# A linear-attention kernel with a two-layer block: transposes of q and k moved from TensorE to crossbar DMA, a scheduler that models the DMA queue, and one token chunk loaded between the halves of a weight

## The chip, the cores and the metric

One core of one Trainium2 chip. The metric is the device time of one execution in microseconds (us); a profiled execution also gives a span, from its first to its last instruction, some 2 to 5 us shorter than the times of the unprofiled runs. Ratios compare kernels that ran in turn on the same chip.

The core's engines are TensorE (PE in the profile; PEld is its weight load), VectorE (DVE), ScalarE (ACT), GpSimd (POOL) and SyncE (SP), which here only issues transfers. "SPq" is SyncE's in-order queue of transfers. The core has two on-chip memories: here TensorE's results land in PSUM and are copied from there to SBUF, where the other operands lie. "The mask" below is VectorE's multiplication of the scores by the causal mask.

## The reference

Batch 4, 8 heads, 768 positions, head size 64. Decaying linear attention by blocks, then two dense layers with a smooth rectifier between them:

```python
for b in range(nb):                       # blocks of 64 positions
    intra = einsum('bhic,bhjc->bhij', qb, kb) * Dmask
    intra = einsum('bhij,bhjd->bhid', intra, vb)
    inter = einsum('bhid,bhde->bhie', qb * lam_pow, kv_state)
    out[:, :, sl] = intra + inter
    kv_state = lam_block * kv_state + einsum('bhsd,bhse->bhde', kb * rev_pow, vb)
x = out.transpose(0, 2, 1, 3).reshape(3072, 512)
h = x @ w_in                              # 512 x 2048
g = where(h >= 1, h, where(h <= -1, 0, (h + 1)**2 / 4))
y = g @ w_out                             # 2048 x 512
```

## The kernel before

The 3072 tokens are 24 chunks of 128 (six per batch element), and four chunks make a stripe of 512. Each chunk is loaded as three transfers of 256 KB (k, q, v), cast to bf16 with the decay factor multiplied in, transposed, and taken through scores (`s`), mask (`m`), output (`o`) and state update (`u`). Each stripe then goes through layer one (`l1`), the rectifier (`r` on ScalarE, `g` on VectorE) and layer two (`l2`).

Casts, transposes and the copies out of PSUM that follow them:

```python
def cast(c, x, eng):                      # eng: GpSimd, except four casts of the first chunks
    tab, d, nm = ((tab_q, qs, "qs"), (tab_k, ks, "ks"))[x]
    t = qkp.tile([128, H, D], BF16, name=nm, tag=nm)
    eng.tensor_tensor(t, qkv_ld[c, x], _bc(tab[:, c % NCB, :], 2, D), op=AX.mult)

def f_t(c):                               # 8 transposes on TensorE
    ptt[c] = pp_t.tile([128, 2, HP, 128], BF16, name="pt", tag="pt")
    for i, x in ((1, ks), (0, qs)):
        for hp in range(HP):
            nc.tensor.transpose(out=ptt[c][:, i, hp, :], in_=pair(x[c], hp), identity=ident)

def f_kb(c, hi):
    nc.vector.tensor_copy(kbd[c % NKB][HD[hi], :, hi, :], ptt[c][HD[hi], 1])

def f_qT(c, e):
    qT[c] = qtp.tile([128, HP, 128], BF16, name="qT", tag="qT")
    (nc.scalar.copy if e == "ACT" else nc.vector.tensor_copy)(qT[c], ptt[c][:, 0])
```

The program is not written in its final order. Each step is an operation with an engine, an assumed duration, needs and a due time; a list scheduler (`run_plan`), run when the kernel is built, puts them in order. Before, a transfer is an operation of a made-up engine "DMA" that does one at a time:

```python
add(("ld", i, x), "DMA", 1190, ..., [("cast", i - LD, x), ...], extra=1400, due=pos_)
...                                       # loads: chunks 0-3, w_in (4 quarters), chunk 4, w_out (4), the rest
t, e = min((max(free[e], min(r for r, _ in lst)), e) for e, lst in ready.items() if lst)
free[e] = t + x.ns
x.t, x.end = t, t + x.ns + x.extra
```

## Time and profile before

| | before |
|---|---|
| median of 4 runs | 239.69 us (238.71 to 240.53) |
| span of the profiled execution | 234.8 us |
| TensorE, VectorE, GpSimd busy | 213.8, 160.3, 59.4 us |
| TensorE waits after 50 us that the profile names | 1.5 us |
| DMA engines full until | about 123 us |

The lines behind this are in the prediction below. How to read such a page: busy time is the union of an engine's instructions and says only how full it is. Whether time there is worth anything is decided by the windows (is the engine full in that stage?) and by the waits (what ended its idle time?). Matmul records can be missing (before: 1876 recorded, 1904 weight loads), so a small hole in TensorE is a wait only if the list of waits names it.

### The profile page before, as it was taken

The page shows a single profiled execution, that of the slowest core. Times are in us where ns is not written, and L with a number is a line of the kernel's source. Part 1 is how long each engine was busy: PE and PEld are TensorE (multiplying, and loading weights), DVE is VectorE, ACT ScalarE, POOL GpSimd, SP SyncE. Part 2 cuts the span into 40 slices and gives each one's busy share as a digit, 9 for nine tenths or more (in the row PEclk, how much of TensorE's full clock was granted, in tenths as well). Part 3 has the DMA queues.
Part 4 walks back from the last instruction along what each step waited for, and adds up shares of the span by engine and source line. Part 5 has one row for each costly group of instructions (what it writes and reads, how often), then busy time and mean ns, then how long its engine had stood idle before and what let it go on. Part 6 is the DMA issues. An engine that isn't in the chain of part 4 may idle for free.

```text
span 234.8 us, 4665 instructions
## 1 busy us (share of the span) xinstructions
PE 213.8 (91%) x1876; PEld 137.1 (58%) x1904; DVE 160.3 (68%) x274; ACT 123.4 (53%) x216; POOL 59.4 (25%) x64
## 2 busy tenths in 40 slices
PE   0487997999997999999999999999999999999993
PEld 0476633575896997777765455555555454444441
DVE  7587399957499999885776876876766835545300
ACT  3456566243577766666566366566455354544110
POOL 6562071061366548303303403302000000000000
PEclk9999999999999999999999999999999999999999
DMA  6999969986999999899993011011011011110212
GB/s 139 220 212 200 192 112 185 196 162 186 247 201 218 227 221 206 191 243 228 230 255 81 19 45 37 12 45 47 0 45 47 0 45 47 45 43 2 92 51 83
DMA packets 82725, 29.67 MB, mean 126 GB/s; under 512 B 75536, under 2 KB 79632, under 8 KB 82704
## 3 DMA queue, kind: packets, MB, share of 16 engines
q1 hardware_dynamic: 78336, 25.17, 48.2%
q0 software_dynamic: 4224, 4.19, 11.1%
q8 instruction: 15, 0.25, 0.4%
q14 instruction: 6, 0.05, 0.1%
q10 hardware_dynamic: 144, 0.00, 0.0%
HBM read 27.27 MB, written 6.29 MB: 143 GB/s over the span
## 4 chain that ended last, share of the span: by engine, by line
PE 75%; DVE 16%; ACT 3%; DMA 2%; issue 2%; SPq 0%; ACTq 0%
PE py L323 33%; PE ph L295 26%; PE ps L252 5%; DVE gT L315 4%; PE pt L229 4%; PE po L268 4%; DMA x2f<-in_v_dram 2%; DVE sc L258 2%; PE pu L242 2%; PE po L265 2%; ACT r L303 1%; DVE kbd_121 L232 1%; PE ph L288 1%; DVE kbd_120 L232 1%; DVE qT L236 1%
## 5 line engine op out<-in xcount | busy, mean ns | idle before, releaser
L303 ACT ACTIVATE r<-ph,one 128x512 bf16<-128x512 f32 x94 | 64.1, 687 | 57.6 <-PE ph L295 40.9
L295 PE MATMUL ph<-xT,w_in_sb 128*128 128x128 bf16 (+1 forms) x744 | 93.1, 269 | 1.0 <-ACT r L303 0.4
L323 PE MATMUL py<-w_out_sb,gT 128*128 128x512 bf16 x364 | 91.5, 379 | 0.9
L295 PEld LDWEIGHTS <-w_in_sb 128*128 128x128 bf16 x752 | 53.0, 98 | 28.0 <-issue 1.4
L323 PEld LDWEIGHTS <-gT 128*128 128x128 bf16 x384 | 35.4, 98 | 33.3 <-DVE gT L315 0.2
L219 POOL TENSOR_TENSOR ks<-x1f,tab_k 128x512 bf16<-128x512 f32 x21 | 24.0, 1141 | 93.0 <-DMA x1f<-in_k_dram 38.9
L258 DVE TENSOR_TENSOR sc<-ps,causal 128x512 bf16<-128x512 f32 x48 | 33.0, 687 | 19.0 <-PE ps L252 18.8
L219 POOL TENSOR_TENSOR qs<-x0f,tab_q 128x512 bf16<-128x512 f32 x23 | 25.8, 1123 | 7.0 <-DMA x0f<-in_q_dram 6.9
L328 ACT COPY osb<-py 128x512 f32<-128x512 f32 x24 | 14.1, 586 | 20.6 <-PE py L323 20.0
L275 ACT CAST xT<-po 128x512 bf16<-128x512 f32 x24 | 14.0, 585 | 11.9 <-PE po L268 11.8
L242 PEld LDWEIGHTS <-ks 128*128 128x128 bf16 x80 | 6.2, 105 | 9.7 <-DVE ks L219 7.1
L229 PE MATMUL pt<-ident,ks 128*128 128x128 bf16 x96 | 10.1, 232 | 0.1
L229 PE MATMUL pt<-ident,qs 128*128 128x128 bf16 x96 | 10.0, 231 | 0.0
L229 PEld LDWEIGHTS <-ks 128*128 128x128 bf16 x96 | 7.7, 106 | 3.3 <-issue 0.3
L252 PE MATMUL ps<-qT,kbd_121 128*128 128x128 bf16 x64 | 6.8, 229 | 3.0 <-DVE qT L236 1.7
L242 PE MATMUL pu<-vi_126,ks 128*128 128x128 bf16 x24 | 2.5, 232 | 7.7 <-ACT vi_126 L223 7.7
L236 DVE COPY qT<-pt 128x512 bf16<-128x512 bf16 x20 | 8.5, 425 | 0.3
L252 PEld LDWEIGHTS <-kbd_121 128*128 128x128 bf16 x64 | 4.9, 102 | 5.8 <-DVE kbd_121 L232 2.6
L252 PE MATMUL ps<-qT,kbd_120 128*128 128x128 bf16 x64 | 6.8, 229 | 1.4 <-ACT qT L236 1.1
L232 DVE COPY kbd_120<-pt 64x512 bf16<-64x512 bf16 x16 | 6.7, 418 | 1.7 <-PE pt L229 0.9
L252 PE MATMUL ps<-qT,kbd_122 128*128 128x128 bf16 x64 | 6.5, 225 | 1.3 <-DVE qT L236 0.8
L252 PEld LDWEIGHTS <-kbd_120 128*128 128x128 bf16 x64 | 4.8, 102 | 3.8 <-DVE kbd_120 L232 1.8
(207 smaller groups left out, 246.4 us busy)
## 6 DMA issues: line engine op xcount, KB each, us to landing
x1f<-in_k_dram SPq DMA_DIRECT2D x24, 256.0 KB, 4.6
x0f<-in_q_dram SPq DMA_DIRECT2D x24, 256.0 KB, 4.8
x2f<-in_v_dram SPq DMA_DIRECT2D x24, 256.0 KB, 4.7
out_dram<-osb SPq DMA_DIRECT2D x24, 256.0 KB, 2.0
w_in_sb<-in_moe_w_in_dram POOLq DMA_DIRECT2D x4, 512.0 KB, 8.3
w_out_sb<-in_moe_w_out_dram POOLq DMA_DIRECT2D x4, 512.0 KB, 8.3
lam_b<-in_lam_dram ACTq DMA_DIRECT2D x1, 4.0 KB, 3.3
```

The costliest lines, as they stand in the source:

```text
L219: eng.tensor_tensor(t, qkv_ld[c, x], _bc(tab[:, c % NCB, :], 2, D), op=AX.mult)
L229: nc.tensor.transpose(out=ptt[c][:, i, hp, :], in_=pair(x[c], hp), identity=ident)
L232: nc.vector.tensor_copy(kbd[c % NKB][HD[hi], :, hi, :], ptt[c][HD[hi], 1])
L236: (nc.scalar.copy if e == "ACT" else nc.vector.tensor_copy)(qT[c], ptt[c][:, 0])
L242: nc.tensor.matmul(pu[0][:, hp, :], lhsT=pair(ks[c], hp), rhs=v_pair(vi[c % NV], hp), start=(c % NCB == 0 and hp == 0), stop=True, skip_gr ...
L252: nc.tensor.matmul(pst[c, g][:, 2 * j + hi, :], lhsT=kbd[c % NKB][:, 2 * g + j, hi, :], rhs=qT[c][:, 2 * g + j, :], start=True, stop=True)
L258: nc.vector.tensor_tensor(sc_sb[c][:, 4 * g:4 * g + 4, :], pst[c, g], _bc(causal, 1, 4), op=AX.mult)
L275: nc.scalar.copy(out=xT[sx][:, :, off:off + C], in_=pot[c])
L295: nc.tensor.matmul(ph[:, j * m:(j + 1) * m], lhsT=w_in_sb[:, ko, (ni + j) * 128:(ni + j + 1) * 128], rhs=xT[s][:, ko, part * m:(part + 1) ...
L303: nc.scalar.activation(out=r_t[grp][:, i, :], in_=ph_t[s, ni, part], func=AF.Relu, bias=one[:, 0:1])
L323: nc.tensor.matmul(py_t[s, ms], lhsT=gT[s][:, ko, ms * 128:(ms + 1) * 128], rhs=w_out_sb[:, ko, :], start=(ko == 0), stop=(ko == FO - 1))
L328: nc.scalar.copy(out=osb[s, ms], in_=py_t[s, ms])
```

## The change

Five things, meant to take work off TensorE and to let the scheduler judge when a transfer lands:

1. Chunks 6 to 23 (`XT = 6`) are transposed by the DMA crossbar (a transfer that writes its data transposed), two transfers of 128 KB per chunk, issued by SyncE. Their `qT` copy goes; the two half copies of `kbd` read SBUF.
2. The scheduler models the queue: SyncE issues (`SP`, with its own time), at most three transfers of it are unfinished (`RING = 3`), all share one DMA time line.
3. Chunk 4's loads move from behind `w_in` to between its halves, and the second half of `w_in` is issued after the cast of chunk 4's k.
4. TensorE's order in stripe 0 is fixed (`seq0`); one group of scores gets another PSUM bank; three early parts of layer one instead of four.
5. Four instead of three buffers for the cast and the transposed q and k.

```diff
+    XT, NQT, NQK, RING = 6, 4, 4, 3
+    ORDER = [(0, 0), (0, 1), 4, (0, 2), (0, 3), (1, 0), (1, 1), (1, 2), (1, 3)]
...
+            self.extra = dma + 2700 - ns if dma else extra
...
+            t, e = min((max(free[e], min(r for r, _ in lst), xfer[-RING] if e == "SP" else 0), e)
+                       for e, lst in ready.items() if lst)
...
+            if x.dma:
+                dma_free = max(dma_free, t + 1300) + x.dma
+                x.end = dma_free + 1400
+                if e == "SP":
+                    xfer.append(dma_free)
...
     def f_kb(c, hi):
-        nc.vector.tensor_copy(kbd[c % NKB][HD[hi], :, hi, :], ptt[c][HD[hi], 1])
+        nc.vector.tensor_copy(kbd[c % NKB][HD[hi], :, hi, :], ptt[c][HD[hi], 1] if c < XT else kT[c][HD[hi]])
+    def f_kx(c):
+        kT[c] = qtp.tile([128, HP, 128], BF16, name="kT", tag="kT")
+        nc.sync.dma_start_transpose(out=kT[c], in_=ks[c].rearrange("p h d -> p (h d)"))
+    def f_qx(c):
+        qT[c] = qtp.tile([128, HP, 128], BF16, name="qT", tag="qT")
+        nc.sync.dma_start_transpose(out=qT[c], in_=qs[c].rearrange("p h d -> p (h d)"))
...
+            add(("t", c), "SP", 1200, lambda c=c: f_kx(c), [...], due=-2, dma=860)
+            add(("qT", c), "SP", 1200, lambda c=c: f_qx(c), [...], due=-2, dma=860)
...
+    for x, y in zip(seq0, seq0[1:]):
+        OPS[y].keys.append(x)
```

More of the change, by code (lines that the diff above doesn't have):

```diff
@@ L62 @@
     ld = ctx.enter_context(tc.tile_pool(name="ld", bufs=LD))
-    qkp = ctx.enter_context(tc.tile_pool(name="qkp", bufs=3))
-    qtp = ctx.enter_context(tc.tile_pool(name="qtp", bufs=3))
+    qkp = ctx.enter_context(tc.tile_pool(name="qkp", bufs=NQK))
+    qtp = ctx.enter_context(tc.tile_pool(name="qtp", bufs=NQT))
     scp = ctx.enter_context(tc.tile_pool(name="scp", bufs=3))
@@ L155, with __init__, add @@
     class Op:
-        def __init__(self, key, eng, ns, fn, needs, due, extra):
-            self.key, self.eng, self.ns, self.fn, self.keys, self.own, self.extra = key, eng, ns, fn, needs, due, extra
-    def add(key, eng, ns, fn, needs=(), due=None, extra=0):
-        OPS[key] = Op(key, eng, ns, fn, needs, due, extra)
+        def __init__(self, key, eng, ns, fn, needs, due, extra, dma):
+            self.key, self.eng, self.ns, self.fn, self.keys, self.own, self.dma = key, eng, ns, fn, needs, due, dma
+            self.extra = dma + 2700 - ns if dma else extra
+    def add(key, eng, ns, fn, needs=(), due=None, extra=0, dma=0):
+        OPS[key] = Op(key, eng, ns, fn, needs, due, extra, dma)
         ops.append(OPS[key])
@@ L178, in run_plan @@
         for x in reversed(topo):
-            d = [u.due - u.ns - x.extra - LAT for u in users[x.key] if u.eng != "DMA"]
+            d = [u.due - u.ns - x.extra - LAT for u in users[x.key] if not u.dma]
             x.due = min(d + ([x.own] if x.own is not None else []), default=1e9)
-            if x.eng == "DMA" or x.key[0] in ("l1", "l2"):
+            if x.dma or x.key[0] in ("l1", "l2"):
                 x.due = x.own
@@ L187, in run_plan @@
                 ready[x.eng].append((0, x))
-        out_seq = []
+        out_seq, xfer, dma_free = [], [0] * RING, 0
         while len(out_seq) < len(ops):
-            t, e = min((max(free[e], min(r for r, _ in lst)), e) for e, lst in ready.items() if lst)
+            t, e = min((max(free[e], min(r for r, _ in lst), xfer[-RING] if e == "SP" else 0), e)
+                       for e, lst in ready.items() if lst)
             r, x = min(((r, x) for r, x in ready[e] if r <= t), key=lambda p: (p[1].due, p[0]))
@@ L206, in mm @@
         return sum(c / 2.4 + 3 for c in cols)
-    qs, ks, qT, sc_sb, xT, ptt, pst, pot = {}, {}, {}, {}, {}, {}, {}, {}
+    qs, ks, kT, qT, sc_sb, xT, ptt, pst, pot = {}, {}, {}, {}, {}, {}, {}, {}, {}
     pu = [None]
@@ L248, in f_s @@
     def f_s(c, g):
-        pst[c, g] = pp_s.tile([128, 4, 128], F32, name="ps", tag="ps")
+        pl, nm = (pp_h, "ph") if (c, g) == (CPS - 1, 1) else (pp_s, "ps")
+        pst[c, g] = pl.tile([128, 4, 128], F32, name=nm, tag=nm)
         for j in range(2):
@@ L283, in f_l1 @@
             if split == 0:
-                pl, nm = (pp_h, "ph") if ni < 2 else (pp_y, "py")
+                pl, nm = (pp_h, "ph") if ni == 0 else (pp_y, "py")
                 ph_t[s, ni, part] = pl.tile([128, MS], F32, name=nm, tag=nm)
@@ L367, in f_load @@
         qkv_ld[c, x] = t
-    order = [("c", c) for c in range(CPS)] + [("w", 0), ("c", CPS), ("w", 1)] + [("c", c) for c in range(CPS + 1, NCH)]
-    pos_ = 0
-    for kind, i in order:
-        if kind == "w":
-            for j in range(WS):
-                add(("wi", i, j), "POOL", 900, lambda i=i, j=j: (load_w_in, load_w_out)[i](j),
-                    [("cast", CPS - 2 + min(j, 1), 0), ("cast", CPS - 2 + min(j, 1), 1), ("wi", i, j - 1)] if i == 0 else [("cast", CPS, 1), ("cast", CPS, 0) if j else None, ("wi", i, j - 1)],
-                    due=j + 4 * i)
-                add(("w", i, j), "DMA", 3100, lambda: None, [("wi", i, j), ("ld", CPS - 1, 2) if i == 0 else ("ld", CPS, 1)], extra=1500, due=pos_)
-                pos_ += 1
+    order = list(range(CPS)) + ORDER
+    order += [c for c in range(CPS, NCH) if c not in order]
+    w_seen, last_c, pos_ = [], None, 0
+    for it in order:
+        if isinstance(it, tuple):
+            lead = [("cast", CPS - 2, 0), ("cast", CPS - 2, 1)] if not w_seen else [("cast", last_c, 1)]
+            add(("w",) + it, "POOL", 900, lambda it=it: (load_w_in, load_w_out)[it[0]](it[1]),
+                lead + [("w",) + w_seen[-1]] if w_seen else lead, due=pos_ * 1e-3, dma=3100)
+            w_seen.append(it)
+            pos_ += 1
             continue
+        gated = len(w_seen) - 2 if last_c is not None and w_seen and not isinstance(order[order.index(it) - 1], int) else None
         for x in (1, 0, 2):
-            wait = {CPS: WS - 2, CPS + 1: 2 * WS - 2}.get(i) if x == 1 else None
-            add(("ld", i, x), "DMA", 1190, lambda i=i, x=x, wait=wait: f_load(i, x, wait),
-                [("cast", i - LD, x), ("w", int(i > CPS), WS - 2) if i >= CPS else None], extra=1400, due=pos_)
+            add(("ld", it, x), "SP", 590, lambda i=it, x=x, wait=gated if x == 1 else None: f_load(i, x, wait),
+                [("cast", it - LD, x), ("w",) + w_seen[-2] if w_seen else None], due=pos_ * 1e-3, dma=1190)
             pos_ += 1
+        last_c = it
     for c in range(NCH):
@@ L393 @@
                 lambda c=c, x=x, eng=(nc.vector if e == "DVE" else nc.gpsimd): cast(c, x, eng),
-                [("ld", c, x), ("t", c - 3), ("u", c - 3), ("cast", c - 1, x)])
+                [("ld", c, x), ("cast", c - 1, x), ("t", c - NQK), ("u", c - NQK) if x else ("qT", c - NQK)])
         add(("cast", c, 2), "ACT", 640, lambda c=c: cast_v(c),
             [("ld", c, 2), ("o", c - NV), ("u", c - NV), ("cast", c - 1, 2)])
-        add(("t", c), "PE", mm(*[128] * 8), lambda c=c: f_t(c),
-            [("cast", c, 0), ("cast", c, 1), ("kb", c - 1, 0), ("kb", c - 1, 1), ("qT", c - 1)], due=od - 6000, extra=FILL)
+        if c < XT:
+            add(("t", c), "PE", mm(*[128] * 8), lambda c=c: f_t(c),
+                [("cast", c, 0), ("cast", c, 1), ("kb", c - 1, 0), ("kb", c - 1, 1), ("qT", c - 1)], due=od - 6000, extra=FILL)
+            e = "ACT" if c < CPS else "DVE"
+            add(("qT", c), e, 600 if c < CPS else 365, lambda c=c, e=e: f_qT(c, e), [("t", c), ("o", c - NQT), ("qT", c - 1)])
+        else:
+            add(("t", c), "SP", 1200, lambda c=c: f_kx(c), [("cast", c, 1), ("kb", c - NQT, 0), ("kb", c - NQT, 1)], due=-2, dma=860)
+            add(("qT", c), "SP", 1200, lambda c=c: f_qx(c), [("cast", c, 0), ("o", c - NQT)], due=-2, dma=860)
         for hi in range(2):
-            add(("kb", c, hi), "DVE", 365, lambda c=c, hi=hi: f_kb(c, hi), [("t", c), ("s", c - NKB, 1)])
-        e = "ACT" if c < CPS else "DVE"
-        add(("qT", c), e, 600 if c < CPS else 365, lambda c=c, e=e: f_qT(c, e), [("t", c), ("o", c - 3), ("qT", c - 1)])
+            add(("kb", c, hi), "DVE", 365 if c < XT else 285, lambda c=c, hi=hi: f_kb(c, hi), [("t", c), ("s", c - NKB, 1)])
         if cb < NCB - 1:
@@ L409 @@
             add(("s", c, h), "PE", mm(*[128] * 4), lambda c=c, h=h: f_s(c, h),
-                [("kb", c, 0), ("kb", c, 1), ("qT", c), ("m", c, 0) if h else ("m", c - 1, 1)],
+                [("kb", c, 0), ("kb", c, 1), ("qT", c), (("m", c, 0) if c != CPS - 1 else None) if h else ("m", c - 1, 1) if c != CPS else ("m", c - 1, 0)],
                 due=od - 3000 + 1000 * h, extra=FILL)
@@ L421 @@
     l2_order = [x for x in l_seq if x[0] == 2]
-    NA = 4
+    NA = 3
     for i in range(NA):
@@ L433 @@
             lambda a=(s, i, n, p, 1 if n1 < NA else None): f_l1(*a),
-            kx + [("w", 0, (i + n - 1) * WS // FO), ("la", n1) if n1 < NA else ("r", n1 - (4 if n1 < NA + 2 else 2)), ("l1", n1 - 1)], due=l_due[1, s, i, p], extra=FILL)
+            kx + [("w", 0, (i + n - 1) * WS // FO), ("la", n1) if n1 < NA else ("r", 0 if n1 == NA + 1 else n1 - 2) if n1 > NA else ("m", CPS - 1, 1), ("l1", n1 - 1)], due=l_due[1, s, i, p], extra=FILL)
         add(("r", n1), "ACT", 690, lambda a=(s, i, n, p, grp, j): f_r(*a),
@@ L449 @@
             add(("y", y), "ACT", 600, lambda a=(s, ms): f_y(*a), [("l2", n2), ("y", y - 1), ("st", y - 3)])
-            add(("st", y), "DMA", 780, lambda a=(s, ms): f_st(*a), [("y", y), ("st", y - 1)], extra=1400, due=-1)
-    run_plan({"PE": 7000, "ACT": 6500, "DVE": 6000, "POOL": 7000, "DMA": 2000})
+            add(("st", y), "SP", 550, lambda a=(s, ms): f_st(*a), [("y", y), ("st", y - 1)], due=-1, dma=780)
+    seq0 = [("u", 0), ("t", 0), ("s", 0, 0), ("t", 1), ("s", 0, 1), ("u", 1), ("o", 0)]
+    for c in range(1, CPS):
+        seq0 += [("s", c, 0), ("t", c + 1), ("s", c, 1)] + ([("u", c + 1)] if c < CPS - 2 else []) + [("o", c)] if c < CPS - 1 else [
+            ("s", c, 0), ("s", c, 1), ("la", 0), ("la", 1), ("o", c), ("la", 2), ("l1", 0), ("l1", 1), ("l1", 2), ("l1", 3), ("u", c)]
+    for x, y in zip(seq0, seq0[1:]):
+        OPS[y].keys.append(x)
+    run_plan({"PE": 7000, "ACT": 6500, "DVE": 6000, "POOL": 7000, "SP": 800})
 _INS = ['q', 'k', 'v', 'lam', 'moe_w_in', 'moe_w_out']
```

## The prediction

> **What bounds the kernel now.** I read the page's first two parts, then the windows by stage, then the waits of TensorE, and last the timelines of TensorE and of the two queues that issue transfers. The page of the kernel before says this (engines with busy time, share and count; then forty slices of 5.87 us each, in tenths):
>
> ```profile
> span 234.8 us, 4665 instructions
> PE 213.8 (91%) x1876; PEld 137.1 (58%) x1904; DVE 160.3 (68%) x274; ACT 123.4 (53%) x216; POOL 59.4 (25%) x64
> ...
> PE   0487997999997999999999999999999999999993
> ...
> DMA  6999969986999999899993011011011011110212
> GB/s 139 220 212 200 192 112 185 196 162 186 247 201 218 227 221 206 191 243 228 230 255 81 19 45 37 12 45 47 0 45 47 0 45 47 45 43 2 92 51 83
> ```
>
> TensorE is full from about the eighth slice to the end, the DMA engines are full only up to slice 21, some 123 us. So two things are busy together in the first half and only one in the second. Which of them sets the end is seen in the windows (busy time and count for PE, PEld, DVE, ACT, POOL; then clock, DMA share, GB/s):
>
> ```profile
> 0.00:7.67 7.67, 0.00 (x1) 0.10 (x1) 5.29 (x11) 2.48 (x5) 5.67 (x13) 1.00 0.81 159
> 7.67:20.00 12.33, 9.63 (x85) 8.48 (x85) 8.76 (x15) 6.66 (x14) 6.49 (x8) 1.00 1.32 212
> 20.00:30.00 10.00, 8.33 (x80) 5.63 (x81) 4.58 (x9) 5.60 (x11) 0.00 (x0) 1.00 1.12 197
> 30.00:50.00 20.00, 17.93 (x142) 10.43 (x143) 17.33 (x28) 10.13 (x17) 7.66 (x8) 1.00 0.98 174
> 50.00:70.00 20.00, 19.89 (x244) 15.27 (x244) 14.75 (x24) 11.42 (x21) 7.94 (x8) 1.00 0.92 194
> 70.00:80.00 10.00, 8.72 (x139) 7.89 (x138) 9.74 (x18) 7.06 (x14) 5.47 (x5) 1.00 1.00 212
> 80.00:140.00 60.00, 59.06 (x659) 42.95 (x668) 48.82 (x86) 36.46 (x66) 20.04 (x18) 1.00 0.81 177
> 140.00:220.00 80.00, 79.53 (x493) 41.64 (x501) 51.02 (x89) 41.20 (x68) 6.13 (x6) 1.00 0.09 34
> ```
>
> From 50 us on TensorE has hardly a hole. Part of the 1.28 us missing in 70 to 80 is not a wait: groups of w_out matmuls stand there as three records where the program has four. The waits say it better: from 50 to 230 us TensorE waits 1.5 us in all (0.8 for qT, 0.5 and 0.2 for sc, all three made by VectorE). Between 20 and 50 us it waits 3.8 us, of which this is the largest item:
>
> ```profile
> PE ps L252 <- DVE qT L236: 1.7, 1, 1.7
> ```
>
> From 7.67 us (first matmul) to 20 us it is short of work and its 128-column matmuls come 107 ns apart rather than 56. At the end some 4 us go by after the last matmul (last copy, last store). So the kernel is: about 8 us of start, 40 us with holes, 180 us of TensorE without holes, 4 us of tail. The transfers are full but ahead: the last load is issued at 120.8 us, while the last transposes of these data run at 181.9 us.
>
> **What the Trainium skill says.** "TensorE: Matmul & The Clock Gate", § Wait — 56ns, not 53.3ns?, gives N/2.4 GHz + 2.5 ns for warm back-to-back matmuls, 55.6 ns at 128 columns and 215.7 at 512, and 106.7 ns for 128 columns cold. The trace agrees: four 128-column transposes start 0.22 us before what follows, four 512-column matmuls take 0.86 us, and the cold groups before 19 us take 0.43 us for four. "VectorE: DVE Perf Modes", § The three transpose paths, puts a 128x128 bf16 transpose at 390 ns on TensorE against 1309 ns by the DMA crossbar; the trace before has no crossbar transpose, and its TensorE transposes, pipelined, cost a seventh of the 390. "DMA: Bandwidth & Descriptors", § Latency and other measured facts, gives 261 GB/s for DMA transposes with a non-contiguous middle dimension; no run here shows it yet. The VectorE page, § Why PSUM operands drop a tier, says that a PSUM operand keeps a copy out of the mode that uses both SBUF read ports. Here copies out of PSUM take 0.42 us for 512 columns; the SBUF form is not in the trace.
>
> **The change part by part.**
>
> *Transposes off TensorE.* Chunks 6 to 23, 18 of 24, no longer use it for transposing. The rows of the removed work and of the copies after it:
>
> ```profile
> L229 PE MATMUL pt<-ident,ks 128*128 128x128 bf16 x96 | 10.1, 232 | 0.1
> L229 PE MATMUL pt<-ident,qs 128*128 128x128 bf16 x96 | 10.0, 231 | 0.0
> L236 DVE COPY qT<-pt 128x512 bf16<-128x512 bf16 x20 | 8.5, 425 | 0.3
> ```
>
> The 232 ns is the latency of one, and the 20 us busy time counts it overlapped; what TensorE gains is the spacing, 56 ns. Removed are 18 x 8 = 144 transposes, 144 x 0.0558 = **8.0 us**. All of these lie after 50 us in the order of the old program, where TensorE waits for nothing, so they come off the end almost whole. (They are the last 144 of 192, the later six-eighths.)
>
> *VectorE.* 18 copies of qT go (18 x 0.425 = 7.7 us). The 36 half copies of kbd stay, but read SBUF; if they fall from 0.42 to 0.29 us, the number that the new scheduler assumes, that is 36 x 0.13 = 4.7 us. Together 12 of 160 us. VectorE is not the bound, but it is 97% busy from 70 to 80, and the 1.5 us of TensorE waits after 50 us are all on it. I take **0.8 us** from this.
>
> *Transfers added.* 36 transposes of 128 KB each. At the page's 261 GB/s one is 0.5 us; the scheduler in the diff assumes 0.86 us of transfer and 1.2 us on the issuing queue. I estimate 36 x 0.86 = 31 us of DMA and 43 us of queue. Loads now pass at about one per 1.1 to 1.2 us, so a chunk costs 3.6 us of DMA now, and some 5.3 us plus a store (2 us to landing) after. TensorE uses a stripe of four chunks per some 33 us in the second half, 8 us per chunk. So the transfers, spread to some 150 us instead of 123, still run ahead. The narrow place is chunks 8 to 12: the old kernel consumes them between 79 and 98 us, 4.7 us each, faster than 5.3 us; but it casts chunk 8 at 64 us, a lead of 15 us. I charge **1.5 us** for new waits, mostly here.
>
> *Start.* Chunk 4's loads come after the first half of w_in, not the whole. Before, they are issued at 26.5 us, when the third quarter has landed:
>
> ```profile
> 26.50 0.37 SPq L364 DMA_DIRECT2D x1f<-in_k_dram  x1
> 26.91 0.58 SPq L364 DMA_DIRECT2D x0f<-in_q_dram  x1
> 27.54 1.40 SPq L364 DMA_DIRECT2D x2f<-in_v_dram  x1
> 43.87 0.37 SPq L364 DMA_DIRECT2D x1f<-in_k_dram  x1
> ```
>
> Weights land some 3.1 us apart (my estimate from first issue at 14.1 us and third landing at 26.4), so the first quarter is in at about 20.2 us and chunk 4 arrives some 5 us earlier. That can remove the 1.7 us wait at 40 us. The price: quarters three and four of w_in are issued after the cast of chunk 4's k, so I estimate the third at 31 to 32 us; the ninth block of the first layer, which reads it, starts at 31.4 us now. Order on TensorE in stripe 0 hardly changes: score group two of chunk 3 gets another PSUM bank, three early parts instead of four, one state update put back. Of 3.8 us waited in 20 to 50, I take **1.8 us** net.
>
> *Sum:* 240.1 - 8.0 - 0.8 - 1.8 + 1.5 = **231.2 us**, 3.7% less.
>
> **Rivals.** (1) *The queue becomes the wait.* Loads, stores and transposes share one in-order queue; a transpose waiting for a cast holds the loads behind it. For it: even before, the queue stands from 48.3 to 53.2 us on a store with a load behind. Against it: six load buffers and the lead of 15 us. If transposes cost double (2 us each of queue and DMA), a chunk is some 8 us, about what TensorE needs, and chunks 8 to 12 come late by 5 to 8 us: 236 to 239 us. (2) *The late w_in half stalls stripe 0.* That would eat the gain of the start and up to 3 us more: 233 to 235. (3) *Hidden anyway:* if something other than TensorE set the pace after 50 us, removing the transposes would give nothing, some 239; the 1.5 us of waits speak strongly against it. (4) *All works,* with the holes of 20 to 80 us closed too: 228.
>
> **Range and chances.** The arithmetic of the 8.0 us is firm; the terms around it are each 1 to 3 us. The range is 228 to 236.5 us. "Faster by over 2%" begins below 235.3 us, so the new waits may eat up to four of the nine microseconds: chance 0.83. Within 2%: 0.14, mainly rival 1. Slower: 0.03, if transposes take several microseconds each.
>
> **What would show it.** Right: TensorE with 144 fewer matmuls and some 300 fewer instructions with their weight loads, still full from 50 us on; span near 226; DMA full until 145 to 155 us; VectorE near 148 us; half copies of kbd clearly under 0.42 us. Wrong: TensorE waits on kbd or qT of chunks 6 to 12 summing to several us, or slices 9 to 16 of TensorE under 9; a wait on w_in near 31 us; transposes that take over 1.5 us each of queue or of DMA; VectorE copies no shorter.

## More of the kernel before

The rectifier on VectorE has three instructions for each group of 1024 columns, all with operands in SBUF only; the mask reads PSUM:

```python
nc.vector.tensor_scalar(t, r, 0.5, 1.0, op0=AX.mult, op1=AX.min)
nc.vector.tensor_tensor(w, r, t, op=AX.subtract)
nc.vector.tensor_tensor(gT[...], w, t, op=AX.mult)
...
nc.vector.tensor_tensor(sc_sb[c][:, 4*g:4*g+4, :], pst[c, g], _bc(causal, 1, 4), op=AX.mult)   # mask
```

## The result

The changed kernel takes **232.22 us** (median of 4 runs, 231.14 to 233.71) against 239.69; its result is correct. The ratio is 0.9694, 95% interval 0.9625 to 0.9764. A ratio is the mean time of one kernel's runs over that of the other's of the same rounds, so not quite the ratio of the medians. Executions over 1.5% slower than the fastest of the same kernel are left out of the means. Run again on another chip (first experiment below) the ratio was 0.9739 (0.9696 to 0.9782). So the change saves 6 to 7.5 us.

The page of the changed kernel, the lines that answer to those of before:

```profile
span 229.4 us, 4429 instructions
PE 207.1 (90%) x1756; PEld 127.4 (56%) x1756; DVE 159.9 (70%) x256; ACT 123.5 (54%) x216; POOL 63.3 (28%) x64
...
PE   0497969999999998988999998999999999999993
...
DMA  6999599997796999699989898998211011110212
```

TensorE has 148 fewer weight loads (144 transposes and 4 of the early parts), and 6.7 us less busy time. The DMA engines are full to slice 28 (160 us), where before they were to slice 21. And one number stands out against the prediction: VectorE is busy for 159.9 us, as before, though it has 18 instructions fewer.

The windows of the changed kernel from 70 us on (busy time and count of PE, PEld, DVE, ACT, POOL; clock, DMA share, GB/s):

```profile
70.00:80.00 10.00, 9.98 (x111) 7.03 (x109) 8.15 (x13) 6.10 (x12) 4.18 (x4) 1.00 0.95 220
80.00:140.00 60.00, 56.54 (x656) 41.66 (x654) 50.06 (x79) 38.81 (x69) 22.14 (x20) 1.00 0.98 199
140.00:220.00 80.00, 79.11 (x461) 39.50 (x459) 49.96 (x83) 40.83 (x68) 9.58 (x7) 1.00 0.33 81
```

The hole of 70 to 80 us is closed (9.98 against 8.72), but 80 to 140 has a new one (56.54 of 60 against 59.06). TensorE's waits, first in 20 to 50 us, then from 50 us on (engine, line, what it waited for: us in total, times, longest):

```profile
PE ph L313 <- DMA w_in_sb<-in_moe_w_in_dram: 2.0, 1, 2.0
...
PE ps L270 <- DVE sc L276: 2.9, 5, 0.8
PE po L286 <- DVE sc L276: 0.9, 2, 0.7
PE pu L259 <- ACT vi_127 L232: 0.7, 1, 0.7
```

After 50 us it waits 4.5 us instead of 1.5, of which 3.8 us are for VectorE's mask. The crossbar itself is named nowhere among them. Its cost, from the views of one tile (issue time on the queue in ns, minimum/median/maximum) and the transfers' time to landing:

```profile
L249 SPq DMA_TRANSPOSE kT<-ks x18: 1205/1340/2855, 53.7 to 159.2; - x18
L241 DVE COPY kbd_122<-kT x12: 272/288/292, 73.7 to 166.9; 64x512 bf16<-64x512 bf16 x12
...
DMA to landing us min/median/max: 2.4/3.6/4.8
```

A transpose holds the queue for 1.2 us or more (median 1.34 for k, 1.21 for q). What it costs the 16 DMA engines comes from the queue's line on the page (packets, MB, share of the engines' time), before and changed:

```profile
q1 hardware_dynamic: 78336, 25.17, 48.2%
q1 hardware_dynamic: 97920, 29.90, 62.0%
```

That is 48.2% of 234.8 us before and 62.0% of 229.4 us now; the difference, 142.2 - 113.2 = 29 us, over 36 transposes is 0.81 us each. The half copy of `kbd` fell from 0.42 to 0.29 us.

**Where the time went,** from a mark that both programs have, ScalarE's copies of finished output rows. The first starts at 52.6 us before and 51.7 after: 0.9 us from the start. The sixteenth, after which no attention work is left, starts at 187.8 and 182.7: 5.1 us. The rest runs alike. So between the two marks 4.2 us are won: 8.0 us of transposes less 3.0 us of added waits would be 5.0, and 0.8 us is left over. An estimate for most of it: a wait is listed from a matmul's modelled end, 0.22 us after its start, where the next could have started 0.056 us after, so each wait is some 0.16 us longer than listed. The changed kernel lists eight after 50 us, the kernel before four: 0.6 us.

These two traces differ by 5.4 us of span, the medians by 7.5 us: the profiled execution of the kernel before (236.49 us) was 3.2 us faster than its median, that of the changed kernel (231.14 us) 1.1 us. So the account covers the 5.4.

**Why VectorE did not get shorter.** A stretch of VectorE's timeline in the changed kernel (start, us, ...):

```profile
99.58 1.41 DVE L331 TENSOR_TENSOR w_1621<-r,t_1619 128x1024 bf16<-128x1024 bf16 x1
101.03 0.69 DVE L333 TENSOR_TENSOR gT<-w_1621,t_1619 128x1024 bf16<-128x1024 bf16 x1
101.64 0.68 DVE L276 TENSOR_TENSOR sc<-ps,causal 128x512 bf16<-128x512 f32 x1
102.24 1.04 DVE L329 TENSOR_SCALAR t_1686<-r 128x1024 bf16<-128x1024 bf16 x1
103.31 0.69 DVE L331 TENSOR_TENSOR w_1688<-r,t_1686 128x1024 bf16<-128x1024 bf16 x1
104.04 1.41 DVE L333 TENSOR_TENSOR gT<-w_1688,t_1686 128x1024 bf16<-128x1024 bf16 x1
```

and GpSimd's in the same time:

```profile
99.22 1.23 POOL L228 TENSOR_TENSOR qs<-x0f,tab_q 128x512 bf16<-128x512 f32 x1 [2.52 <-DMA x0f<-in_q_dram]
101.95 1.04 POOL L228 TENSOR_TENSOR ks<-x1f,tab_k 128x512 bf16<-128x512 f32 x1 [1.50 <-PE pu L259]
103.65 1.25 POOL L228 TENSOR_TENSOR qs<-x0f,tab_q 128x512 bf16<-128x512 f32 x1 [0.66 <-DMA x0f<-in_q_dram]
```

The same instruction takes 0.69 us, or 1.41 where a cast on GpSimd started just before it. Set the ends side by side: the first cast ends at 100.45 and the delayed `w` at 100.99; the third cast ends at 104.90 and the delayed `gT` at 105.45. In the two traces, before and changed, each of the 49 operations that a cast delayed ends a fixed time after that cast, whenever it began: 0.55 us for `w` and `gT`, 0.28 for `t`, 0.15 for `kbd`. So it does not run slowly beside the cast, it waits until the cast has ended. I counted after 26 us, for `t`, `w`, `gT` and `kbd` from SBUF, those that overlap a cast and those that are slow, that is, take over 0.05 us more than their usual time (0.43, 0.69, 0.69, 0.29 us):

| | overlap a cast | of these slow | other | of these slow | time above usual |
|---|---|---|---|---|---|
| before | 31 | 19 | 113 | 0 | 9.7 us |
| changed | 52 | 30 | 127 | 2 | 20.7 us |

The two others begin near 28 us, while GpSimd issues the transfers of the weights. The mask, which reads PSUM, overlaps casts too (19 times before, 14 after) and is never slow. So the 12 us that VectorE saved came back as 11 us of delay. Why more overlaps: the casts of k and q now come one by one as their loads land (GpSimd's wait for q's load rose from 6.9 to 20.5 us), later in the run. That VectorE has more instructions that read SBUF only, the `kbd` copies, explains little: of the 30 delayed two are `kbd`, nine `t`, eight `w` and eleven `gT` (before: thirteen, three and three of the last three kinds). The reason for the number stays argued; that the casts cause the delay is tested below.

### The profile page after: what moved, and what is told of

Its sections match the earlier page's. It is cut to its first block, busy times and chain, and to the rows that moved or that the text cites. A ratio compares the mean times of both kernels' runs of the same rounds, so it can differ in the third digit from the quotient of the medians.

```text
span 229.4 us, 4429 instructions
## 1 busy us (share of the span) xinstructions
PE 207.1 (90%) x1756; PEld 127.4 (56%) x1756; DVE 159.9 (70%) x256; ACT 123.5 (54%) x216; POOL 63.3 (28%) x64
## 4 chain that ended last, share of the span: by engine, by line
PE 63%; DVE 30%; DMA 2%; ACT 2%; issue 1%; SPq 0%; ACTq 0%
PE py L341 32%; PE ph L313 21%; DVE gT L333 8%; DVE sc L276 6%; PE ps L270 4%; PE po L286 3%; DMA x2f<-in_v_dram 2%; DVE kbd_121 L241 1%; PE po L283 1%; DVE kbd_120 L241 1%; PE pu L259 1%; PE pt L238 1%; ACT r L321 1%; DVE w_2199 L331 1%; DVE w_2313 L331 1%
## 5 line engine op out<-in xcount | busy, mean ns | idle before, releaser
L341 PE MATMUL py<-w_out_sb,gT 128*128 128x512 bf16 x384 | 93.3, 379 | 0.0
L341 PEld LDWEIGHTS <-gT 128*128 128x128 bf16 x384 | 35.9, 98 | 35.8 <-DVE gT L333 0.2
L276 DVE TENSOR_TENSOR sc<-ps,causal 128x512 bf16<-128x512 f32 x47 | 32.3, 687 | 18.7 <-PE ps L270 18.3
L228 POOL TENSOR_TENSOR ks<-x1f,tab_k 128x512 bf16<-128x512 f32 x21 | 25.2, 1201 | 68.5 <-DMA x1f<-in_k_dram 33.5
L228 POOL TENSOR_TENSOR qs<-x0f,tab_q 128x512 bf16<-128x512 f32 x23 | 28.3, 1230 | 29.2 <-DMA x0f<-in_q_dram 20.5
L293 ACT CAST xT<-po 128x512 bf16<-128x512 f32 x24 | 14.1, 586 | 11.7 <-PE po L286 11.7
L259 PEld LDWEIGHTS <-ks 128*128 128x128 bf16 x80 | 6.1, 102 | 10.9 <-DVE ks L228 7.6
L270 PE MATMUL ps<-qT,kbd_120 128*128 128x128 bf16 x60 | 6.4, 229 | 2.9 <-DVE sc L276 1.6
L270 PE MATMUL ps<-qT,kbd_121 128*128 128x128 bf16 x64 | 6.8, 225 | 2.1 <-DVE sc L276 1.3
L270 PEld LDWEIGHTS <-kbd_121 128*128 128x128 bf16 x64 | 4.8, 100 | 5.5 <-issue 2.1
L270 PEld LDWEIGHTS <-kbd_120 128*128 128x128 bf16 x64 | 4.8, 102 | 5.4 <-issue 2.3
L270 PE MATMUL ps<-qT,kbd_122 128*128 128x128 bf16 x64 | 6.3, 219 | 0.3 <-DVE sc L276 0.3
L263 ACT CAST ubd_124<-pu 64x256 bf16<-64x256 f32 x16 | 5.8, 365 | 1.0 <-PE pu L259 0.8
L263 ACT CAST ubd_123<-pu 64x256 bf16<-64x256 f32 x16 | 5.8, 365 | 0.8 <-PE pu L259 0.7
L270 PEld LDWEIGHTS <-kbd_122 128*128 128x128 bf16 x64 | 4.7, 98 | 2.7 <-issue 0.4
L283 PE MATMUL po<-qT,ubd_123 128*128 128x128 bf16 x32 | 5.9, 219 | 0.0
L283 PE MATMUL po<-qT,ubd_124 128*128 128x128 bf16 x32 | 5.9, 219 | 0.0
```

What stands on the lines that cost most here:

```text
L259: nc.tensor.matmul(pu[0][:, hp, :], lhsT=pair(ks[c], hp), rhs=v_pair(vi[c % NV], hp), start=(c % NCB == 0 and hp == 0), stop=True, skip_gr ...
L263: nc.scalar.copy(out=ubd[c % NUB][HD[hi], :, HD[hi]], in_=pu[0][HD[hi], :, HD[hi]])
L270: nc.tensor.matmul(pst[c, g][:, 2 * j + hi, :], lhsT=kbd[c % NKB][:, 2 * g + j, hi, :], rhs=qT[c][:, 2 * g + j, :], start=True, stop=True)
L276: nc.vector.tensor_tensor(sc_sb[c][:, 4 * g:4 * g + 4, :], pst[c, g], _bc(causal, 1, 4), op=AX.mult)
L283: nc.tensor.matmul(po[:, hp], lhsT=ubd[(c - 1) % NUB][:, hp, :], rhs=qT[c][:, hp, :], start=True, stop=False)
L293: nc.scalar.copy(out=xT[sx][:, :, off:off + C], in_=pot[c])
```

## The experiments

Twelve kernels, five rounds each. How much faster or slower a run is than the changed kernel is taken against the changed kernel, by the ratios to the kernel before, in us of about 238. The intervals make such a difference uncertain by some 1.5 us, and the chips differ too. Wherever an edit changes what the scheduler reads, it may order everything anew; only the tenth and eleventh runs keep the plan of the changed kernel.

| run | ratio to before | 95% interval | first mark, 16th mark in the trace (us) |
|---|---|---|---|
| before (trace) | 1 | | 52.6, 187.8 |
| changed again | 0.9739 | 0.9696 to 0.9782 | 51.6, 183.6 |
| no crossbar | 1.0042 | 0.9995 to 1.0090 | 51.2, 190.3 |
| w_in before chunk 4 | 0.9864 | 0.9822 to 0.9906 | 51.2, 186.3 |
| casts off GpSimd (wrong result) | 0.9592 | 0.9553 to 0.9632 | 51.9, 179.9 |
| free order in stripe 0 | 0.9762 | 0.9725 to 0.9799 | 52.4, 183.7 |
| old queue model | 0.9942 | 0.9898 to 0.9985 | 52.2, 186.8 |
| chunk 4 after three quarters | 0.9853 | 0.9810 to 0.9897 | 53.4, 185.6 |
| stores from ScalarE, rescheduled | 0.9858 | 0.9805 to 0.9911 | 51.2, 187.0 |
| no crossbar, old queue model | 1.0049 | 1.0014 to 1.0085 | 52.1, 189.7 |
| casts in halves | 0.9721 | 0.9686 to 0.9757 | 52.0, 182.4 |
| stores from ScalarE, same plan | 0.9967 | 0.9926 to 1.0008 | 51.7, 188.4 |
| halves, third quarter earlier | 0.9642 | 0.9592 to 0.9692 | 51.0, 182.9 |

### 1. The changed kernel again

No edit.

> The changed kernel itself, run again on the chip of the following runs, so that they can be set against it. Expected 0.965 to 0.975 of the kernel before, VectorE near 160 us busy, one TensorE wait of about 2 us on w_in near 31 us.

Measured 231.81 us against 237.76. VectorE 157.9 us; the wait on `w_in` was 1.0 us this time. After 50 us TensorE waited 3.0 us for the mask and 2.4 us for v's copy, which needs v's load. This is the yardstick for what follows.

### 2. The crossbar alone undone

```diff
-    XT, NQT, NQK, RING = 6, 4, 4, 3
+    XT, NQT, NQK, RING = 24, 4, 4, 3
```

> All parts of the change but the crossbar: every chunk is transposed on TensorE, with the new start and the new scheduler. Theory A (the gain is TensorE time removed, 144 transposes x 0.056 = 8.0 us, less about 3 us of new TensorE waits on VectorE): this run loses 5 to 8 us against the changed kernel, so 0.99 to 1.00 of the kernel before. Rival B (most of the gain comes from the start and the scheduler): it keeps most of it, 0.975 to 0.985. On VectorE: theory A also says that the slow operations come with the casts on GpSimd, so they may fall back towards the count of before (22 operations, 9.7 us extra) as the work between changes.

(The expectation says 22 slow operations of before; the count is 19.) Measured 238.98 us, 7.2 us slower than the changed kernel, at the upper end of what theory A gave and outside rival B: all of the net gain needs the crossbar. Slow operations overlapping a cast fell to 16, time above usual to 11.7 us. The start is as good as in the changed kernel (first mark 51.2 us), but it is lost again before 100 us; the window of 70 to 80 us:

```profile
70.00:80.00 10.00, 8.69 (x125) 7.19 (x123) 9.71 (x18) 6.16 (x12) 5.47 (x5) 1.00 1.03 192
```

VectorE is 97% busy at 70 to 80 us again, with the copies out of PSUM back, and TensorE waits 3.8 us for the mask from 65 to 95 us. So VectorE's relief is real in this stage: it is part of the 7.2 us.

### 3. Chunk 4 behind the whole of w_in

```diff
-    ORDER = [(0, 0), (0, 1), 4, (0, 2), (0, 3), (1, 0), (1, 1), (1, 2), (1, 3)]
+    ORDER = [(0, 0), (0, 1), (0, 2), (0, 3), 4, (1, 0), (1, 1), (1, 2), (1, 3)]
```

> Crossbar and scheduler kept; only the place of chunk 4's loads undone: all four quarters of w_in ahead of it. Theory: the 2.0 us wait of TensorE on w_in at 30 us goes, a wait of 1 to 2 us on chunk 4 near 38 to 40 us comes back; so within 1 us of the changed kernel, either way. Rival: the early chunk 4 is worth what I booked, 1.8 us net: this run is 1.8 us or more slower than the changed kernel.

Measured 234.92 us, 3.1 us slower: my theory (within 1 us) fell, the rival's "1.8 us or more" stands. TensorE's timeline shows why a wait of 2 us costs more than 2 us (start, us, ..., idle before and what ended it):

```profile
41.62 0.23 PE L270 MATMUL ps<-qT,kbd 128*128 128x128 bf16 x1 [1.98 <-DVE kbd L241]
42.08 0.34 PE L270 MATMUL ps<-qT,kbd 128*128 128x128 bf16 x3 [0.23 <-DVE kbd L241]
42.26 2.88 PE L341 MATMUL py<-w_out_sb,gT 128*128 128x512 bf16 x8
44.93 0.63 PE L270 MATMUL ps<-qT,kbd 128*128 128x128 bf16 x4
```

Eight matmuls of 512 columns take 2.7 us up to the next start, where they take 1.73 elsewhere: after the wait the granted clock fell (0.91 as the mean of 30 to 50 us, 0.50 from 44 to 46). The Trainium skill, "TensorE: Matmul & The Clock Gate", § What's actually happening, describes a free-running activity window of 3413 ns that halves the clock after an idle window. The trace agrees in kind, but here an idle time of 2.0 us was enough. The changed kernel's wait of 2.0 us on `w_in` did not do it. The clocks in the traces show why. In every trace the changes of the clock lie whole multiples of 3.41 us apart, so its first rise to full fixes a grid. In this trace the wait lies inside one stretch of the grid, 39.59 to 43.01 us, and the whole next stretch is at half clock:

```profile
43.01:46.42 3.41, 3.38 (x19) 1.88 (x17) 2.27 (x4) 0.00 (x0) 0.00 (x0) 0.50 1.06 213
```

The changed kernel's wait (30.46 to 32.43 us) lies across a border, 31.45, and so does the 2.4 us of run 1 (100.10 to 102.45, border 101.10). Over all 14 traces, four stretches between the first rise and the last matmul had TensorE idle for 1.97 us or more, two in this trace (the other, before 121.51 us, with a wait of 2.1 us for v's copy) and one each in runs 7 and 12; each was followed by 3.41 us at half clock, some 1.7 us of work. No other stretch, up to 1.94 us idle in run 5, was. How much of the 3.1 us is the clock is open: among this run's six executions one at a granted clock of 0.998 took 234.98 us, no less than the others.

### 4. The casts taken off GpSimd (wrong result)

```diff
-        eng.tensor_tensor(t, qkv_ld[c, x], _bc(tab[:, c % NCB, :], 2, D), op=AX.mult)
+        if eng is None:
+            nc.scalar.copy(out=t, in_=qkv_ld[c, x])          # no decay factor
+        else:
+            eng.tensor_tensor(t, qkv_ld[c, x], _bc(tab[:, c % NCB, :], 2, D), op=AX.mult)
...
+            e = "ACT" if c >= XT else e
```

> Wrong result on purpose: from chunk 6 on the casts of k and q are plain copies on ScalarE, without the decay factor, so GpSimd does nothing beside VectorE's work; transfers and crossbar stay. Theory C (VectorE's operations that read SBUF only are held up while GpSimd runs a tensor_tensor): slow operations after 60 us fall from some 28 to at most 3, VectorE busy falls from 160 to 149 us or less, TensorE's waits for sc after 50 us fall from 3.8 us to 1 us or less, and the time falls by 1 to 3 us if ScalarE, 23 us busier, does not become a wait. Rival D (the slow operations come from the crossbar's or the loads' writes into SBUF): they stay, as those transfers stay, and VectorE keeps some 158 us.

(The changed kernel's count of slow operations is 32 after 26 us and 25 after 60 us, not 28.) Measured 228.35 us, 3.5 us faster than the changed kernel. That is more than the 1 to 3 us that theory C expected. All transfers and the crossbar stay, though the scheduler may order them anew. Its window of 80 to 140 us:

```profile
80.00:140.00 60.00, 57.85 (x646) 41.60 (x645) 40.40 (x77) 46.91 (x87) 0.00 (x0) 1.00 1.12 201
```

VectorE is busy for 40.4 us there instead of 50.1, 142.7 us in all; 4 slow operations are left in the whole run and 3.2 us above usual, and TensorE waits for no mask after 50 us. Theory C holds and rival D, that writes of the transfers into SBUF slow VectorE, falls. The Trainium skill has this rule: "SBUF — State Buffer", § Who interferes with whom, says that a VectorE instruction with two SBUF inputs, or in a mode that uses both ports, and a GpSimd instruction that reads SBUF, as the casts do, exclude each other, and that one with at most one SBUF input outside these modes does not contend. This agrees: `w` and `gT` have two SBUF inputs, `t` and the `kbd` copy have one, and all are delayed; the mask (PSUM and SBUF) never. I had not used the rule in the prediction. One limit: the copies on ScalarE are also shorter (0.62 us) than the casts (1.2 us) and the order is a new one, so a part of the 3.5 us may be that. The delay itself does not rest on this run alone, as the fixed ends in the changed kernel's trace show it too.

### 5. Free order in stripe 0

```diff
-    for x, y in zip(seq0, seq0[1:]):
-        OPS[y].keys.append(x)
```

> Only the fixed order of stripe 0 undone, the scheduler is free there; all else as changed. In the traces of the changed kernel TensorE's first layer starts at 21.2 to 21.7 us against 22.7 before, and its clock is full some 4 us earlier. Theory: the fixed order is worth that 1 to 1.5 us, so this run is 0.5 to 1.5 us slower than the changed kernel. Rival: the gain of the start is all in chunk 4's loads (3 us by the third run), and the fixed order is worth nothing: equal within 0.5 us.

Measured 232.33 us, 0.5 us slower, intervals overlapping: the fixed order is worth 0.5 us at most as far as this shows. The first mark is 0.7 to 0.8 us later. Inconclusive, and small.

### 6. The old picture of the transfers in the scheduler

```diff
-        xfer[-RING] if e == "SP" else 0
+        0
...
+            if dma and eng == "SP":
+                self.ns = ns = max(ns, dma)
...
-                dma_free = max(dma_free, t + 1300) + x.dma
-                x.end = dma_free + 1400
-                if e == "SP":
-                    xfer.append(dma_free)
+                if e == "SP":
+                    x.end = t + x.ns + 1400
+                else:
+                    dma_free = max(dma_free, t + 1300) + x.dma
+                    x.end = dma_free + 1400
```

> Only the scheduler's picture of the transfers undone: a transfer from the in-order queue takes its time on the queue and lands 1.4 us later, with no limit of three in flight and no shared DMA time. Crossbar, start and loads' places are kept. Theory: the model matters where queue order decides when a chunk's data arrive, so this run shows more TensorE waits after 50 us (over 6 us in all against 4.5 to 5.6) and is 1 to 4 us slower than the changed kernel. Rival: the order of the queue has room to spare and the time is the same within 0.7 us.

This picture is close to that of the kernel before but not the same: there the weights took their turns on the same made-up engine as the loads, here they have a time line of their own. Measured 236.56 us: 4.8 us slower by the ratios, slightly more than the theory's 1 to 4. TensorE's waits after 50 us sum to 7.3 us, and now the crossbar is among them:

```profile
PE ps L273 <- DVE sc L279: 2.1, 2, 1.2
PE ps L273 <- DMA qT<-qs: 2.1, 2, 1.5
```

So waits for the crossbar, which rival 1 of the prediction feared, are part of what the new model keeps away (2.1 of the 7.3 us); the first mark is 0.6 us later too. That the transposes stood behind others in the queue is not shown. The transfers are the same; only the order on the queue and the engines differs.

### 7. Chunk 4 after three quarters of w_in

```diff
-    ORDER = [(0, 0), (0, 1), 4, (0, 2), (0, 3), (1, 0), (1, 1), (1, 2), (1, 3)]
+    ORDER = [(0, 0), (0, 1), (0, 2), 4, (0, 3), (1, 0), (1, 1), (1, 2), (1, 3)]
```

> Chunk 4's loads after three quarters of w_in instead of two. Theory: the wait of TensorE on w_in's third quarter near 31 us (1.0 to 2.0 us) goes, and chunk 4 comes about 3 us later than in the changed kernel, in time or late by less than 1 us; so 0.5 to 1.5 us faster than the changed kernel. Rival: chunk 4 is what decides, and the wait moves to it: 1 to 3 us slower, between the changed kernel and the third run.

Measured 234.46 us, 2.7 us slower: a miss. The wait on `w_in` went, but TensorE waited 2.1 us for chunk 4's `kbd` at 40 us, and the clock was at half from 42.0 to 45.4 us. The rival was right. The fall costs time: the two of its six executions at a granted clock of 0.998 or more took 233.3 and 233.9 us, the four at 0.988 to 0.993 took 234.2 to 235.3.

### 8. Stores from ScalarE's queue

```diff
-        nc.sync.dma_start(out=out[m0:m0 + 128, :], in_=osb[s, ms])
+        nc.scalar.dma_start(out=out[m0:m0 + 128, :], in_=osb[s, ms])
...
-            add(("st", y), "SP", 550, ...
+            add(("st", y), "ACT", 400, ...
```

> The stores are issued from ScalarE's queue, so a store that waits for its copy no longer stands before loads and transposes. Rival 1 of the prediction (the one queue becomes the wait) says: TensorE's waits for v's copy (0.7 us in one trace of the changed kernel, 2.4 in another) go, and the time falls by 1 to 3 us. Theory: the waits after 50 us are mostly on VectorE, so it falls by less than 1 us, or ScalarE's issuing costs as much.

Measured 235.09 us (234.75 without the slow execution), 2.8 us slower by the ratios: neither expectation. The wait for v's copy fell to 0.5 us, but those for the mask rose to 6.7 us. As the scheduler had reordered everything, the eleventh run does the same with the order kept.

### 9. No crossbar and the old queue model

The edits of runs 2 and 6 together.

> The fourth corner of a square: no crossbar and the old picture of the transfers, with the new start and buffers kept. The other corners against before: crossbar and new model 0.974, crossbar and old model 0.994, no crossbar and new model 1.004. Theory: the new queue model pays only where transposes share the queue with loads; without them the old one is as good or better, so this run is 0.985 to 1.000 of before, and the start's gain of 1 to 3 us shows here. Rival: the new model is good in itself, and this corner is worst: 1.01 or more.

Measured 238.75 us, 1.0049 of before: outside my range by a little, and not the rival's 1.01. With it the square is full (its corners come from three chips, so each difference is uncertain by some 1.5 us): the crossbar brings 7.2 us (3.0%) with the new model and 2.5 us (1.1%) with the old; the new model brings 4.8 us with the crossbar and nothing without. And without the crossbar the new start with its other buffers brings no net gain.

### 10. Casts in halves

```diff
-        eng.tensor_tensor(t, qkv_ld[c, x], _bc(tab[:, c % NCB, :], 2, D), op=AX.mult)
+        for h in ([slice(0, 4), slice(4, 8)] if c >= XT else [slice(0, 8)]):
+            eng.tensor_tensor(t[:, h], qkv_ld[c, x][:, h], _bc(tab[:, c % NCB, h], 2, D), op=AX.mult)
```

> Correct result. From chunk 6 on each cast on GpSimd is two instructions of four heads; the plan is the same. If a VectorE operation that reads only SBUF is held for as long as one GpSimd instruction runs (0.73 us of the 1.04 us), halves hold it for half as long: extra time on VectorE falls from 19 to 21 us to 10 to 14 us, and the time by 0.5 to 1.5 us against the changed kernel. Rival: two halves collide twice, extra time as before or more, and GpSimd's fixed cost makes the casts late: the same or up to 1 us slower.

Correct result, 231.02 us; 0.9721 against 0.9739, not clear of noise. Of 62 operations that overlap a cast 44 are slow, 14 more than before the edit, but by less each: 16.2 us above usual against 19.0 in run 1, where 10 to 14 were expected; VectorE 154.6 us. The halves are not half as long:

```profile
L229 POOL TENSOR_TENSOR qs<-x0f,tab_q 128x256 bf16<-128x256 f32 x36 | 28.7, 815 | 19.1 <-DMA x0f<-in_q_dram 19.1
```

815 ns for half of what took 1230 ns in the mean; the undisturbed ones take 0.61 us where whole casts take 1.04. TensorE's waits for the mask after 50 us fell to 1.4 us in this trace (three, the longest 0.6 us), but one for v's copy of 1.5 us stood there.

### 11. Stores aside, same plan

Only the first edit of run 8.

> The stores are issued from ScalarE, and the order of everything else is that of the changed kernel (the eighth run let the scheduler reorder all). If the store's place in the queue costs time (rival 1), the wait of TensorE for v's copy near 101 us (0.7 and 2.4 us) goes and the time falls by 0.5 to 2 us. If it stays the same within 0.7 us, the loss of the eighth run came from the reordering and the queue has room; if it is 2 us or more slower, issuing on ScalarE itself costs.

Measured 236.90 us, 5.4 us slower than the changed kernel: the third of the three outcomes. TensorE's waits for the mask rose to 8.3 us:

```profile
PE ps L270 <- DVE sc L276: 5.9, 8, 1.6
PE po L286 <- DVE sc L276: 2.4, 4, 1.1
```

Time above usual on VectorE was 22.7 us. A store's issue takes ScalarE 0.34 us, and with the stores gone the queue's transfers may start at other times than planned. Which of the two makes the masks late is not settled. What it shows is that taking the stores' waits out of the queue made this schedule slower; that it is fitted to the times of its transfers is my reading.

### 12. Halves, and the third quarter of w_in earlier

```diff
+        if i == 2:
+            tc.add_manual_dep(w_dma[2].ins, w_dma[1].ins.name, SYNC)   # wait until the second has landed
...
-else [("cast", last_c, 1)]
+else [("ld", 4, 1) if it == (0, 2) else ("cast", last_c, 1)]
```

on top of run 10.

> Correct result; a version meant to beat both. To the halved casts of the tenth run it adds: the third quarter of w_in is issued when the second has landed, ahead of the cast of chunk 4's k instead of behind it. Chunk 4's loads stay where they are. Theory: the wait of TensorE on w_in (0.7 to 2.0 us in the traces with this order) goes, chunk 4's wait near 36 us stays below 1.5 us, and the time falls by 0.5 to 1.5 us against the tenth run: 0.965 to 0.970 of before. Rival: the third quarter takes DMA time from chunk 4's loads and the wait moves to chunk 4, as in the seventh run: 0.975 or more.

Correct result, 230.57 us against 238.67: **0.9642** (0.9592 to 0.9692), just clear of the 0.9739 (0.9696 to 0.9782) of the changed kernel, but not of the 0.9694 (0.9625 to 0.9764) of its first result. It was run at another time. No wait on `w_in` is left, the first mark is at 51.0 us, and chunk 4's wait is 1.0 us. In the profiled execution a part was lost again:

```profile
101.70 0.54 PE L262 MATMUL pu<-vi,ks 128*128 128x128 bf16 x4 [2.21 <-ACT vi L235]
102.04 1.91 PE L344 MATMUL py<-w_out_sb,gT 128*128 128x512 bf16 x4
```

The wait for v's copy, 2.2 us, was followed by half clock from 101.8 to 105.2 us; the wait of 2.4 us at the same place in run 1, which lay across a border of the grid, was not. This is the clearest measure of what such a fall costs: of the six executions the two at a granted clock of 1.000 took 229.2 us, the two at 0.989 and 0.990 took 231.4 and 231.2. It is the lowest ratio measured; that it beats the changed kernel is likely, not shown.

## Why the prediction was right or wrong

The time, 231.2 us predicted and 232.2 measured, was right. Its terms were not all, and the sum has a slip: 240.1 - 8.0 - 0.8 - 1.8 + 1.5 is 231.0, not 231.2. Of its own signs of being wrong two came, the wait on `w_in` near 31 us and a slice of TensorE under 9 (the sixteenth); of the signs of being right VectorE near 148 us and a span near 226 did not.

- **TensorE is the bound after 50 us: right.** Run 2 puts the transposes back and loses 7.2 us; rival 3 (hidden anyway) is refuted.
- **8.0 us of transposes: right in size.** 144 fewer, and run 2 with them back is 7.2 us slower; between the marks 4.2 us are left after the added waits.
- **VectorE, 12 us shorter and 0.8 us won: the step that failed.** The removed copies and the 0.29 us of the SBUF copies came as reckoned, but I took the rest of VectorE as fixed. In its place, operations that read SBUF only waited longer for casts on GpSimd: time above usual rose from 9.7 to 20.7 us, VectorE stayed at 159.9 us, and TensorE's waits on it rose from 1.5 to 3.8 us instead of falling. Run 4 and the fixed ends in the trace show that the casts are the cause. The relief did show at 70 to 80 us, where the old hole closed; it was spent at 80 to 140.
- **Transfers: the costs were right** (1.2 us of queue, 0.81 us of DMA against 0.86; full until 160 us against "some 150"). **New waits, 1.5 us, mostly at chunks 8 to 12: too small, and wrong in kind.** They grew by 3.0 us. Those that hang on transfers are 0.7 and 2.4 us (two traces), both for v's copy of chunk 13 and none for the crossbar; the rest is the mask. The lead of 15 us was also misread: it runs to chunk 8's output matmuls at 79.0 us, while its scores start at 73.5 and its transposes at 67.9, 4 us after the cast. That no crossbar wait came of it is not to the prediction's credit.
- **Start, 1.8 us net: mis-sized, 0.9 us at the first mark.** I put the third quarter's landing at 31 to 32 us and the need at 31.4; it landed at 32.4, and TensorE, having come there earlier, waited 2.0 us. That is rival 2, in part. A gain that I did not see: TensorE's clock is full from 14.4 us instead of 19.1. What I also missed is the price of the alternative: a late chunk 4 costs some 3 us (runs 3 and 7), in both traces with a fall of the clock.
- **The scheduler's queue model: left out of the sum, and worth 4.8 us.** I charged waits and took it for granted that the order would keep them small. Runs 6 and 9 show that the crossbar brings only 2.5 us without it, each figure give or take 1.5.

That the sum came out is partly luck. It promised 9 us; the two traces differ by 5.4 us, 0.9 short at the start and some 3 short between the marks, and no term was better than booked. The medians differ by 7.5 us, because the profiled execution of the kernel before was a fast one; on the second chip the gain was 6.2 us. All of these lie in the range, but the point that was met belongs to the first pair of medians.

## What to carry to other kernels

Read what an engine's remaining instructions will run beside, not only which instructions it loses: VectorE lost 12 us of work here and gained 11 us of delay from GpSimd. Moving work to an in-order queue pays only if the order on it is planned with its real durations: the same transposes brought 7.2 us with the queue modelled and 2.5 without. And a TensorE wait of about 2 us inside one 3.41 us stretch of the clock's grid was followed by a stretch at half clock, some 1.7 us more, so remove the long ones first.

## What the Trainium skill lacked or had wrong

- "VectorE: DVE Perf Modes", § The three transpose paths, compares 390 ns on TensorE with 1309 ns by crossbar. In a full stream a TensorE transpose costs 56 ns, and the crossbar's cost to the kernel is 1.2 us of queue for 128x512, so the table's figures are not what either path costs in a full schedule.
- "DMA: Bandwidth & Descriptors": its 261 GB/s for DMA transposes was not reached: 0.81 us for 128 KB is 162 GB/s, beside loads in short packets. The time that a transpose on SBUF data holds SyncE's queue, here 1.19 us at least, is given in us for this chip by no page; this one has only cycle counts, of "previous generations".
- "TensorE: Matmul & The Clock Gate" warns of idle gaps over some 3 us. Waits of 2.0, 2.1 and 2.2 us (runs 3, 7, 12) lowered the clock to half; waits of 2.0 and 2.4 us (changed kernel, run 1) did not. What counts in these traces is the idle time inside one 3.41 us stretch of the grid: 1.97 us or more did it, 1.94 did not. The page does not say what share of a window has to be idle.
- "SBUF — State Buffer" has the rule on VectorE and GpSimd and is right; it has no typical size. Here a VectorE instruction of 0.69 us became one of 1.41 us, and ended 0.55 us after the cast that held it.
